# Three key loads of a decode-attention kernel, each issued when a small marker transfer ahead of it has landed

## Chip, cores, metric

One core of one Trainium2 chip. The metric is the device time of one execution in microseconds (us), median of several runs.

## The reference, cut to what matters

Two attention blocks with one query token each (B=4, 32 query heads, 8 key/value heads, head size 128), outputs side by side. Block A reads the whole cache of 8192 positions, block B the last 2048.

```python
q = (x @ wq).reshape(B, 1, 32, 128)                    # per block
scores = einsum("bhqd,bhkd->bhqk", q, k) * 128**-0.5   # k, v: each head serves 4 query heads
p = softmax(scores)
out = einsum("bhqk,bhkd->bhqd", p, v).reshape(B, 1, 4096) @ wo
```

Every key and value is used once, so the bytes of the caches are the work: 184.6 MB are read from HBM in all.

## The kernel before

The work is cut into 20 *units* of 4 MB of keys and 4 MB of values: units 0 to 3 for block B (one batch entry each), 4 to 19 for block A. Keys and values have two buffers each; unit u uses slot u % 2. Between them come 1 MB pieces of the output weights, `Wo`. SyncE issues nearly all transfers, in program order on one queue. Before each it waits until compute has freed the buffer.

```python
def kv_load(kind, u):                       # cut
    ...
    if un["P"] == 1:                        # block B: keys in 2 parts, values in 4 of 1 MB
        for q in range(NPART[kind]):
            ...
            op("sp", dma(buf[:, slot, q * n:(q + 1) * n, :], src), waits=w, inc=(...))
        return
    w = [("otr", u - 2)] if kind == "V" else [("otr", u - 3)] if u >= 2 * T0P else [...]
    ...
    op("sp", lambda sp: sp.sem_inc(sem, bump), waits=w, bump=(sem, bump, None))   # carries the wait
    ...
    op("sp", dma(buf[:, slot, :, :].rearrange("p t d -> p (t d)"), src), inc=(kind, u, 0))

kv_load("K", 0)
for u in range(1, NU + 1):
    if u < NU:
        kv_load("K", u)
    kv_load("V", u - 1)
    tn = u // 2
    if u % 2 == 0 and tn in pieces:         # one Wo piece in two units, u = 6, 8, ... 18
        ...
        op("sp", dma(Wo_sb[...], src), waits=[("ocp", tn - 1)], inc=("wo", tn))
    ...
# then eight loads of 128 KB, the last piece of wo, and the store of the result
```

A wait `("rs", 7)` or `("otr", 5)` is a semaphore wait on the issuing engine; a DMA counts its semaphore up by 16, one from each of the 16 DMA engines.

## Time and profile before

| | before |
|---|---|
| median of 4 runs | 439.17 us (439.14 to 439.53) |
| bytes moved, mean rate | 184.73 MB, 423 GB/s |
| last load landed, profiled run | 434.43 of 437.0 us |

The prediction below shows the slices, the waits and the order of issue. These are the DMA queues of the kernel before (packets, MB, share of the time of 16 engines):

```profile
q1 hardware_dynamic: 10960, 184.56, 99.1%
q8 instruction: 8, 0.13, 0.1%
q14 instruction: 4, 0.03, 0.0%
```

Twelve packets of 16 or 8 KB, a tenth of a per cent, belong to *instruction*: the fetching of the engines' programs. (The packet records have seven of the 16 KB packets between 25 and 71 us, the eighth at 431 us; of the 8 KB ones, one each at 63, 91, 160 and 289 us. Fetches from before the span's start are not on the page.)

### The profile page before, as it was taken

The page shows a single profiled execution, that of the slowest core. Times are in us where ns is not written, and L with a number is a line of the kernel's source. Part 1 is how long each engine was busy: PE and PEld are TensorE (multiplying, and loading weights), DVE is VectorE, ACT ScalarE, POOL GpSimd, SP SyncE. Part 2 cuts the span into 40 slices and gives each one's busy share as a digit, 9 for nine tenths or more (in the row PEclk, how much of TensorE's full clock was granted, in tenths as well). Part 3 has the DMA queues.
Part 4 walks back from the last instruction along what each step waited for, and adds up shares of the span by engine and source line. Part 5 has one row for each costly group of instructions (what it writes and reads, how often), then busy time and mean ns, then how long its engine had stood idle before and what let it go on. Part 6 is the DMA issues. An engine that isn't in the chain of part 4 may idle for free.

```text
span 437.0 us, 15525 instructions
## 1 busy us (share of the span) xinstructions
PE 365.0 (84%) x7174; PEld 337.9 (77%) x7184; DVE 210.0 (48%) x406; ACT 195.0 (45%) x249; POOL 27.7 (6%) x88
## 2 busy tenths in 40 slices
PE   0168898998998959895989598969868996989996
PEld 0158897997997949795979588868868886979975
DVE  0004455664564634563456247525643563455651
ACT  1024473573653625371634254434534462536530
POOL 6100000000000000000000000000100000000000
PEclk9999999999999988999999899989996999799999
DMA  8999999999999999999999999999999999999996
GB/s 340 430 421 421 429 412 430 418 439 412 445 432 432 424 438 432 432 432 432 432 432 429 432 432 430 431 433 432 410 454 432 432 432 432 432 432 411 447 407 255
DMA packets 10996, 184.73 MB, mean 423 GB/s; under 512 B 1236, under 2 KB 2280, under 8 KB 2408
## 3 DMA queue, kind: packets, MB, share of 16 engines
q1 hardware_dynamic: 10960, 184.56, 99.1%
q8 instruction: 8, 0.13, 0.1%
q14 instruction: 4, 0.03, 0.0%
q10 hardware_dynamic: 24, 0.01, 0.0%
HBM read 184.56 MB, written 0.01 MB: 422 GB/s over the span
## 4 chain that ended last, share of the span: by engine, by line
PE 54%; DMA 40%; issue 2%; DVE 1%; SPq 1%; ACT 1%
DMA K_sb<-in_A_k_cache_dram 29%; PE KT L283 27%; PE OT L338 11%; DMA K_sb<-in_B_k_cache_dram 7%; PE SB L322 5%; PE SA L322 4%; DMA V_sb<-in_A_v_cache_dram 4%; PE KT L396 4%; PE SA L350 1%; PE KT L338 1%; SPq L566 1%; DVE oacc L404 1%; PE KT L263 1%; ACT KT_sb L299 1%; DVE OS L501 0%
## 5 line engine op out<-in xcount | busy, mean ns | idle before, releaser
L283 PE MATMUL KT<-identf,K_sb 128*128 128x128 f32 x1280 | 207.6, 296 | 44.1 <-DMA K_sb<-in_A_k_cache_dram 30.7
L299 ACT ACTIVATE KT_sb<-KT 128x1024 bf16<-128x1024 bf16 (+1 forms) x192 | 165.1, 881 | 120.6 <-PE KT L283 120.6
L283 PEld LDWEIGHTS KT<-identf,K_sb 128*128 128x128 f32 x1280 | 147.6, 150 | 49.3 <-DMA K_sb<-in_A_k_cache_dram 31.7
L299 DVE COPY KT_sb<-KT 128x512 int32<-128x512 int32 x160 | 110.5, 691 | 132.1 <-PE KT L283 130.7
L338 PE MATMUL OT<-PT,V_sb 128*128 128x64 bf16 x2560 | 78.1, 193 | 1.6 <-issue 1.1
L338 PEld LDWEIGHTS OT<-PT,V_sb 128*128 128x128 bf16 x2560 | 75.9, 98 | 1.8 <-issue 1.2
L469 ACT ACTIVATE PT<-Dt 128x512 bf16<-128x512 f32 x40 | 24.6, 630 | 84.0 <-DVE Dt L458 84.0
L322 PEld LDWEIGHTS SA<-RQc,KT_sb 128*128 128x128 bf16 x1280 | 56.9, 98 | 2.3
L322 PEld LDWEIGHTS SB<-RQc,KT_sb 128*128 128x128 bf16 x1280 | 51.1, 97 | 7.9 <-issue 4.4
L322 PE MATMUL SA<-RQc,KT_sb 128*128 128x16 bf16 x1280 | 56.4, 170 | 0.0
L322 PE MATMUL SB<-RQc,KT_sb 128*128 128x16 bf16 x1280 | 52.9, 170 | 0.0
L420 DVE TENSOR_REDUCE M<-SB 128x8 f32<-128x512 f32 (+1 forms) x20 | 13.8, 692 | 50.0 <-PE SB L322 50.0
L441 POOL PARTITION_ALL_REDUCE MB<-M1m x20 | 7.7, 387 | 334.3 <-DVE M1m L434 334.3
L396 PE MATMUL KT<-Wo_sb,OL 128*4 128x512 bf16 x80 | 18.9, 379 | 0.0
L201 PE MATMUL KT<-ident,x_sb 4*128 4x4 bf16 x8 | 0.6, 170 | 19.9 <-POOL identf L537 19.9
L201 PEld LDWEIGHTS KT<-ident,x_sb 4*128 4x128 bf16 x8 | 0.4, 112 | 20.1 <-issue 20.1
L476 DVE TENSOR_REDUCE LB<-SA 128x8 f32<-128x512 f32 (+1 forms) x20 | 13.7, 684 | 2.8 <-PE SA L350 2.8
L458 DVE TENSOR_TENSOR Dt<-SA,MBm 128x512 f32<-128x512 f32 x20 | 13.8, 692 | 0.7
L367 DVE TENSOR_TENSOR ORx<-KT,MSK 32x1024 bf16<-32x1024 bf16 x10 | 12.1, 1211 | 3.3 <-PE KT L362 3.3
L458 DVE TENSOR_TENSOR Dt<-SB,MBm 128x512 f32<-128x512 f32 x20 | 13.6, 681 | 0.0
L420 DVE TENSOR_REDUCE M<-SA 128x8 f32<-128x512 f32 (+1 forms) x20 | 13.6, 681 | 0.0
L350 PE MATMUL SA<-PT,onesb 128*128 128x128 bf16 x168 | 12.7, 218 | 0.0
(69 smaller groups left out, 118.0 us busy)
## 6 DMA issues: line engine op xcount, KB each, us to landing
K_sb<-in_A_k_cache_dram SPq DMA_DIRECT2D x15, 4096.0 KB, 22.5
V_sb<-in_A_v_cache_dram SPq DMA_DIRECT2D x15, 4096.0 KB, 30.3
K_sb<-in_B_k_cache_dram SPq DMA_DIRECT2D x8, 2048.0 KB, 23.6
V_sb<-in_B_v_cache_dram SPq DMA_DIRECT2D x16, 1024.0 KB, 18.4
V_sb<-in_B_wq_dram SPq DMA_DIRECT2D x1, 4096.0 KB, 12.5
V_sb<-in_A_wq_dram SPq DMA_DIRECT2D x1, 4096.0 KB, 21.8
Wo_sb<-in_B_wo_dram SPq DMA_DIRECT2D x4, 1024.0 KB, 11.9
K_sb<-in_A_k_cache_dram SPq DMA_DIRECT2D x2, 2048.0 KB, 17.5
```

Source lines behind the costliest of these rows:

```text
L283: ins = pe.transpose(out=bkf[:, pi * 128:(pi + 1) * 128], in_=K_sbf[:, slot, t0:t0 + 2, :].rearrange("p t d -> p (t d)"), identity=identf[ ...
L299: ins = e.tensor_copy(out=d, in_=r) if eng == "dve" else e.activation(out=d, in_=r, func=ACTF.Copy)
L322: ins = pe.matmul(out=stb[:, t % NTH * C:(t % NTH + 2) * C], lhsT=ktv[:, pi, :, e], rhs=RQc[:, u % 2, t // TS, e, :], start=(e == 0), stop ...
L338: ins = pe.matmul(out=otb[:, s * NW:s * NW + w], lhsT=V_sb[:, slot, t, :], rhs=PT[:, slot, t * C:t * C + w], start=(j == 0), stop=(j == n ...
L350: ins = pe.matmul(out=SA[u % 2][:, s * NM:(s + 1) * NM], lhsT=onesb[:, :], rhs=PT[:, u % 2, c0:c0 + NM], start=(i == 0), stop=(i == n - 1))
L367: return dve.tensor_tensor(out=ORx[:, :, :, :], in0=bk[0:NR, 0:128].rearrange("p (i o r) -> p r o i", o=1, r=C).broadcast_to([NR, C, C, 12 ...
L396: ins = pe.matmul(out=bk[0:Bn, 0:D], lhsT=OL[:, i, :], rhs=Wo_sb[:, i, :], start=(i == 0), stop=(i == C - 1))
L420: return dve.tensor_reduce(out=M1[:, h * n:(h + 1) * n].rearrange("p (s h) -> p s h", h=C), in_=bank[:, :].rearrange("p (s j h) -> p s h j ...
L441: return pool.partition_all_reduce(MB[:, 0:n], M1m[:, 0:n], channels=128, reduce_op=ReduceOp.max)
L458: return dve.tensor_tensor(out=Dt[:, h * NTH * C:(h + 1) * NTH * C].rearrange("p (s j h) -> p s j h", s=Sh, h=C), in0=bank[:, :].rearrange ...
L469: return act.activation(out=PT[:, u % 2, a:b], in_=Dt[:, a:b], func=ACTF.Exp, scale=scale)
L476: return dve.tensor_reduce(out=LB[:, 0:n].rearrange("p (s h) -> p s h", h=C), in_=SA[u % 2][:, 0:NSEG * NM].rearrange("p (s j h) -> p s h ...
```

## The change

Three transfers of 1 KB are added. Each stands one 1 MB piece ahead of a key load, and that key load waits until the marker has landed. The intent is to have SyncE issue the key loads of units 5, 9 and 15 at a known place of the stream, with one piece of work still in the queue to cover the way to the first byte.

```diff
+        rs_sb = sb("rs_sb", [16, 32], BF16)
...
+        MARKS = (3, 7, 13)
+        marked = []
+        def mark(u):
+            if u in MARKS:
+                op("sp", dma(rs_sb[:, :], WO[0][0:16, 0:32]), inc=("rs", u))
+                marked.append(u)
+        def passed():
+            return [("rs", marked.pop())] if marked else []
...                                          # block B
-                        w = [("T", tjob_idx[(u - 2, 8 * q + 7)])] if u >= 2 else []
+                        w = ([("T", tjob_idx[(u - 2, 8 * q + 7)])] if u >= 2 else []) + passed()
...
+                        if q == NSEG - 1:   # before the last 1 MB of values
+                            mark(u)
...                                          # block A
-            op("sp", dma(buf[...], src), inc=(kind, u, 0))
+            op("sp", dma(buf[...], src), waits=passed() if kind == "K" else [], inc=(kind, u, 0))
...
             if u % 2 == 0 and tn in pieces:
                 P, q = pieces[tn]
+                mark(u - 1)                 # before the Wo piece
```

More of the change, by code (lines that the diff above doesn't have):

```diff
@@ L128, in bass_concat_heads__gqa_block_cached__sliding_block_cached__decode_kernel @@
                  "out0", "out1", "out2", "Tq", "Td", "Ta", "S", "PV", "Ed", "Ea", "Eq", "vs", "sub", "exp", "otr", "otp",
-                 "ocp", "Ef", "fin0", "fin1", "ar1", "SM", "msk", "pset", "setup", "pm0", "pm1", "oc", "ocB", "mkb", "perm", "rq"]
+                 "ocp", "Ef", "fin0", "fin1", "ar1", "SM", "msk", "pset", "setup", "pm0", "pm1", "oc", "ocB", "mkb", "perm", "rq", "rs"]
         sems = {n: sm("s_" + n) for n in names}
@@ L160, in sem_of @@
             return sems["vs" if t in ("max", "maxc", "sum", "rcp", "os") else t]
-        DMA_KEYS = ("K", "Kh", "KH", "V", "Vh", "VL", "WL", "x", "out", "WQ", "wo")
+        DMA_KEYS = ("K", "Kh", "KH", "V", "Vh", "VL", "WL", "x", "out", "WQ", "wo", "rs")
         plan = {e: [] for e in ("sp", "pe", "act", "dve", "pool")}
@@ L747, in kv_load @@
                 return
-            op("sp", dma(buf[:, slot, :, :].rearrange("p t d -> p (t d)"), src), inc=(kind, u, 0))
+            op("sp", dma(buf[:, slot, :, :].rearrange("p t d -> p (t d)"), src), waits=passed() if kind == "K" else [], inc=(kind, u, 0))
         for P in (1, 0):
```

## The prediction

> **What bounds the kernel now.** I read the page from the top: the busy shares, the slices, the DMA part; then the waits, the issues of SyncE in order of time, and single transfers. The busy shares do not point anywhere by themselves: TensorE is at 84%, VectorE at 48%. The slices do.
>
> ```profile
> PE   0168898998998959895989598969868996989996
> PEclk9999999999999988999999899989996999799999
> DMA  8999999999999999999999999999999999999996
> GB/s 340 430 421 421 429 412 430 418 439 412 445 432 432 424 438 432 432 432 432 432 432 429 432 432 430 431 433 432 410 454 432 432 432 432 432 432 411 447 407 255
> DMA packets 10996, 184.73 MB, mean 423 GB/s; under 512 B 1236, under 2 KB 2280, under 8 KB 2408
> ```
>
> The DMA row is full in 38 of 40 slices, at 432 GB/s, and only the first and the last are not. 184.73 MB at 432 GB/s is 427.6 us of a span of 437.0. TensorE has a hollow (a 5 or 6) in every fourth slice. The waits name it:
>
> ```profile
> PE KT L283 <- DMA K_sb<-in_A_k_cache_dram: 30.7, 8, 5.3
> SPq L566 <- DVE oacc L404: 137.0, 6, 23.8
> SPq L741 <- DVE ON L504: 94.6, 6, 16.5
> ```
>
> TensorE waits for a key load eight times, up to 5.3 us each (once in each pair of units of path A, which takes about 41.3 us). SyncE itself also waits long, for compute to free buffers, and yet the DMA row has no hole. So when SyncE issues there is still work in the ring. The next view is SyncE in order of time, around the second marker (start, duration):
>
> ```profile
> 159.25 0.54 SPq L566 DMA_DIRECT2D K_sb<-in_A_k_cache_dram  x1
> 159.89 0.55 SPq L566 DMA_DIRECT2D V_sb<-in_A_v_cache_dram  x1
> 183.97 0.33 SPq L566 DMA_DIRECT2D Wo_sb<-in_B_wo_dram  x1
> 184.48 0.54 SPq L566 DMA_DIRECT2D K_sb<-in_A_k_cache_dram  x1
> 201.46 0.54 SPq L566 DMA_DIRECT2D K_sb<-in_A_k_cache_dram  x1
> ```
>
> These are the keys of unit 8, values of 7, a piece of Wo (1 MB), keys of 9 and keys of 10; values of 8 (185.12) are left out. The time from issue to landing of three of them, in this order (values of 7, Wo, keys of 9):
>
> ```profile
> DMA to landing us min/median/max: 33.2/33.2/33.2
> ...
> DMA to landing us min/median/max: 11.6/11.6/11.6
> ...
> DMA to landing us min/median/max: 20.8/20.8/20.8
> ```
>
> So they land at 193.1, 195.6 and 205.3: in the order of issue, 2.5 us apart for 1 MB and 9.7 us for 4 MB, whatever the issue time. Counting bytes issued less bytes landed in the packet records, the ring holds 4.3 MB (10 us) when keys 9 are issued, and from the first load to about 410 us it never holds less than 3.06 MB (7.1 us). The kernel is a queue that never runs dry; its length is bytes over rate, plus about 2 us of start and about 3 us of tail.
>
> **What the Trainium skill says.** (1) "DMA: Bandwidth & Descriptors", section "Where 436 GB/s comes from", gives 16 ports at 850 MHz, 435.2 GB/s together. The trace agrees: 432. A packet of 32 KB takes 1211 ns at least, 1218 at the median and 1221 at the ninth decile, so there is no faster transfer to be had. (2) Same page, "Queues, rings and completion order": each of the 16 engines consumes its ring in order. The landings above agree, so a marker lands only when what was issued before it is through. (3) Same page, "Why a DMA increments its semaphore by 16 and not by 1": each engine that takes part counts up by itself, and only the sixteenth increment means landed. The trace shows how far apart they are: the 16 increments of values 7 come from 191.00 to 193.11, those of Wo from 193.50 to 195.59. The skew is a steady 2.1 us. The slowest engine decides. (4) Same page, "Latency and other measured facts", gives about 600 ns from a hardware-generated DMA to its first byte. This trace has more: first issue at 0.80, first packet at 1.84, 1.04 us later.
>
> **The change, part by part.**
>
> *Added instructions.* Three transfers of 16 rows of 64 bytes, one row per engine. A 512-byte packet takes 25 ns and a completion packet of 4 bytes 9 ns, so each marker costs an engine at most about 34 ns, 0.1 us for all three. On SyncE three more issues of about 0.35 us, in time in which it waited anyway.
>
> *Moved: the three key loads.* The order of all big transfers in the ring stays; only the time of issue moves.
> - Marker 1 stands before the fourth 1 MB piece of values 3. The third piece landed at 110.41; keys 5, issued at 98.80, now go out at about 110.5, 11.7 us later.
> - Marker 2 stands behind values 7 and before the Wo piece: keys 9 go from 184.48 to about 193.2, 8.7 us later.
> - Marker 3 stands behind values 13 (landing 317.16): keys 15 go from 308.05 to about 317.2, 9.2 us later.
>
> In each case exactly one piece of 1 MB lies behind the marker, 2.43 us of work. Question: is that enough to cover the way from the marker's landing to the first bytes of the keys?
>
> *The race, for marker 2.* The last engine's completion packet of values 7 is recorded at 192.65, its increment at 193.11 (0.46 later). With the marker's 0.03 and some 0.04 until SyncE goes on (estimate: other issues start 0.02 to 0.05 after the releaser's end), keys 9 issue at 193.18. That slowest engine finishes its share of Wo at 195.14. Slack: 1.96 us.
>
> How long does a transfer on an empty ring need? From the first transfer of the kernel: issued at 0.80, eight 32 KB packets per engine (8 x 1.218 = 9.74 us), increments from 12.52 to 13.32. Less 0.43 us from the last packet to its increment (at the end, 434.00 to 434.43), the data started as if at full rate at 2.35 to 3.15, so 1.55 to 2.35 us after issue, engine by engine. Against 1.96: the early engines' keys are there in time; the latest engine loses 2.35 - 1.96 = 0.39 us. The fast engines, up to 2.2 us ahead (dry at 192.93), do idle, for up to 1.8 to 2.6 us, but that spends their lead and not the end: everything waits for the sixteenth increment. The DMA row could show a small dent and the time nothing.
>
> The other two races have the same terms: last completion packet of the third piece at 109.98, of the fourth at 112.44; of values 13 at 316.69, of the Wo piece at 319.17. Slack about 1.9 to 2.0 us each.
>
> *Sum.* Per marker between 0 (warm, the descriptors come sooner than at the cold start) and 0.4 us; keys 5, 9 and 15 take 0.54 us to issue where the first transfer took 0.39, which might add 0.15 to the upper end. Three times: 0 to 1.6 us, plus 0.1 for the markers. No compute removed, so nothing is won. I take the middle, +0.7 us.
>
> *What is behind on SyncE.* It issues in order, so values 4 (105.95), 8 (185.12) and 14 (308.70) also move, to some 0.6 us after their keys. The next issue is at 123.99, 201.46 and 325.05, at least 7 us later, and waits for compute. With values and keys in the ring as before, the backlog at those points is as before (3.2 to 5.5 MB).
>
> **Rivals.**
> - *Real holes in the ring.* If a marker of 64-byte rows lands 1 us late, or a refill under load takes 3 us, each marker costs about 1.0 to 1.5 us on the slowest engine: +3 to +4.5 us, 442 to 444, still within 2%. For it: the first packets of the cold start took 1.7 to 2.2 us in place of 1.2. Against: the small store at the end lands 1.2 us after its issue, whole.
> - *The fast engines' idling pulls the mean down for good.* All engines move equal bytes; if lead and lag change hands from marker to marker, each hole hits a different slowest engine. The hole of the whole transfer is then the largest lateness, counted above as 0.4 to 0.55 us; at worst 3 x 0.8 = +2.4 us, 441.6.
> - *A gain.* A shallower ring would have to make packets shorter. The minimum lies 0.6% below the median: 2.5 us at the very most, 436.7. Nothing ties packet time to backlog: at 3 and at 10 MB the slices show the same 432 GB/s.
> - *The late keys hurt TensorE.* Keys 9 landed at 205.31 with 10 us in front of them. Unless the ring empties they land at the same time, and TensorE waits for them as before.
>
> **Range and chances.** 439.17 + 0.7 = 439.9 us. The low end, 439.0, is no hole and the best of the noise (439.14 to 439.53); the high end, 441.8, is three holes of about 0.8 us. Two per cent would be 8.8 us, 2.9 us per marker, more than the whole slack plus the refill of a cold start; slower by that 2%, faster 1%, within 2% the rest.
>
> **What would show it.** In the changed profile the keys of 5, 9 and 15 issue at about 110.5, 193.2 and 317, right behind a small transfer, with issue to landing of about 12 us in place of 20.8 to 23.8. Their landings, at 122.6, 205.3 and 329.3, should move by no more than the sum of the holes so far. SyncE should show three waits for the marker's DMA, of 8 to 12 us. The DMA row should stay at 9 and the increments of later transfers should lie closer together than 2.1 us, because the fast engines lost their lead. The prediction is wrong if keys 9 land later than 206.5, if the time falls below 438.5, or if later transfers are issued against an empty ring.

## The result and the profile after

443.01 us, median of 4 runs (442.86 to 443.08), against 439.17: a ratio of 1.0085 (95% interval 1.0068 to 1.0103). It lies within 2%, but outside the predicted range of 439.0 to 441.8. Ratios are the mean time of one kernel's runs over the mean of the other's of the same rounds, so not quite the ratio of the medians.

The page of the changed kernel:

```profile
DMA  8999999999999999999999999999999999999996
GB/s 336 426 425 421 430 413 431 417 438 412 379 428 428 424 441 440 437 398 428 428 428 428 428 428 443 434 443 434 400 414 428 428 428 428 434 431 425 437 421 231
DMA packets 11092, 184.74 MB, mean 419 GB/s; under 512 B 1332, under 2 KB 2376, under 8 KB 2504
```

At this grain there is almost nothing to see. Slices of 11 us still show a 9. Two rates dip at a marker (379 and 398, slices 11 and 18). The third marker's key load goes out at 319.86 us, as slice 30 begins, and that shows only 414; the 400 of slice 29 is no mark of it, since the kernel before has 410 there. The waits show what the change did to SyncE:

```profile
SPq L567 <- DMA rs_sb<-in_A_wo_dram: 30.0, 3, 12.7
PE KT L284 <- DMA K_sb<-in_A_k_cache_dram: 31.1, 10, 5.1
```

Three waits for the marker, 30.0 us in all, and TensorE's wait for keys hardly changed (30.7 us before). SyncE in order of time around the second marker, the same stretch as in the prediction:

```profile
162.41 0.55 SPq L567 DMA_DIRECT2D V_sb<-in_A_v_cache_dram  x1
163.01 0.58 SPq L567 DMA_DIRECT2D rs_sb<-in_A_wo_dram  x1
186.30 0.33 SPq L567 DMA_DIRECT2D Wo_sb<-in_B_wo_dram  x1
194.95 0.54 SPq L567 DMA_DIRECT2D K_sb<-in_A_k_cache_dram  x1
203.81 0.53 SPq L567 DMA_DIRECT2D K_sb<-in_A_k_cache_dram  x1
```

and from issue to landing, for the first four of these (values 7, marker, Wo, keys 9):

```profile
DMA to landing us min/median/max: 32.3/32.3/32.3
...
DMA to landing us min/median/max: 31.9/31.9/31.9
...
DMA to landing us min/median/max: 10.9/10.9/10.9
...
DMA to landing us min/median/max: 12.4/12.4/12.4
```

The landings are at 194.8, 194.9, 197.2 and 207.3. Keys 9 follow Wo by 10.1 us where it was 9.7 before: a hole of 0.4 us, as the prediction had it. Three holes of this size are 1.3 us; the loss is 3.8.

**Sixteen engines, not one queue.** The trace records each of the 16 increments of a transfer's semaphore. Sorted, and less the first of the sixteen, they show how far the engines are apart. Left: when the last one landed (from the traces' semaphore updates, not a view of the profile).

```
before
102.95  0.00 0.07 0.30 0.47 0.70 0.73 0.77 1.48 1.64 1.68 1.72 1.74 1.81 1.93 1.98 2.06   keys 4
154.25  0.00 0.06 0.34 0.50 0.70 0.72 0.78 1.51 1.66 1.69 1.73 1.76 1.81 1.96 2.01 2.09   first Wo piece
163.96  0.00 0.07 0.36 0.51 0.73 0.73 1.43 1.52 1.67 1.71 1.74 1.78 1.83 1.96 2.02 2.10   keys 7
205.31  0.00 0.04 0.29 0.50 0.68 0.70 1.43 1.47 1.65 1.67 1.72 1.75 1.79 1.95 2.01 2.08   keys 9
426.70  0.00 0.26 0.51 0.70 0.72 0.73 1.46 1.51 1.67 1.69 1.74 1.79 1.90 1.98 2.05 2.10   values 19, first part
434.43  0.00 0.46 0.64 0.67 0.68 1.29 1.34 1.47 1.49 1.55 1.59 1.67 1.69 1.78 1.84 1.88   last piece of wo
after
113.60  0.00 0.00 0.02 0.14 0.15 0.88 1.17 1.48 1.55 1.58 1.58 1.66 1.70 1.70 1.71 2.59   values 3, last piece
123.78  0.00 0.05 0.07 0.08 0.14 0.17 0.21 0.23 0.24 0.25 0.28 0.34 0.37 0.45 0.45 0.47   keys 5, first marker
165.56  0.00 0.03 0.03 0.07 0.13 0.16 0.21 0.22 0.23 0.24 0.34 0.35 0.44 0.45 0.46 0.90   keys 7
207.32  0.00 0.01 0.02 0.06 0.06 0.08 0.12 0.14 0.15 0.17 0.20 0.21 0.22 0.23 0.26 0.40   keys 9, second marker
278.31  0.00 0.00 0.01 0.06 0.06 0.08 0.09 0.12 0.14 0.20 0.21 0.21 0.24 0.26 0.41 0.90   values 11
332.23  0.00 0.03 0.21 0.24 0.27 0.31 0.32 0.36 0.38 0.38 0.39 0.40 0.40 0.41 0.42 0.45   keys 15, third marker
436.02  0.00 0.03 0.17 0.18 0.30 0.31 0.32 0.33 0.34 0.35 0.37 0.38 0.40 0.41 0.44 1.86   values 19, last part
438.65  0.00 0.06 0.14 0.16 0.26 0.27 0.28 0.29 0.30 0.31 0.32 0.33 0.34 0.35 0.36 1.58   last piece of wo
```

In the kernel before, six or seven engines run 1.3 to 2.1 us ahead of the slowest, and this *lead* lasts. It costs nothing, since the end is the slowest engine's. It also hides things: the 8 KB instruction packet at 159.76 us falls between the second and the third row, one engine goes from 0.78 to 1.43, and the last landing does not move. In the changed kernel the first marker closes the lead from 2.6 to 0.5 us (*levels* the engines): those that are ahead run dry and wait for the late keys. From then on they march together. And then *single* engines fall behind, by 0.5 us near 163 us, 0.5 near 275 and 1.4 near 434. Each time an instruction packet stands just before. For the last one, the DMA queues of the stretch 433.5 to 435.5 us of the changed kernel, then 431.0 to 432.5 of the kernel before:

```profile
q8 instruction: 1, 0.02, 3.4%
```

```profile
q8 instruction: 1, 0.02, 4.7%
```

Both kernels fetch 16 KB in the tail. The packet takes 1126 ns before and 1080 ns after (packet records); with what it delays around it, it puts one engine back by some 1.4 us. In the kernel before it falls on an engine that is ahead (six engines stand in front in the row of 426.70, five in that of 434.43), and the last landing doesn't move: the last 0.5 MB of values land 1.33 us after the part in front of them, after the change 2.73. The 8 KB packets near 160 and between 274 and 289 us take 309 to 318 ns, and the data packet behind lasts 1565 or 1566 ns (1628 at the later one) in place of 1218, in both kernels: 0.66 to 0.72 us for one engine.

The chain that ended last ends in this. Before, the last 16 matmuls on values run on without a break behind the others (x64 is 48 and these 16); after, TensorE starts them when the delayed engine's increment has come:

```profile
430.48 2.00 PE KT L338 x64
432.48 0.32 issue
432.79 0.27 PE KT L700
```

```profile
411.67 24.35 DMA V_sb<-in_A_v_cache_dram
436.02 0.05 issue
436.06 0.64 PE KT L339 x16
```

**Theory A**, then: a marker's wait costs about 0.4 us of *hole* (time in which even the slowest engine has nothing to move), and it levels the engines; later instruction fetches that fell on engines with a lead now fall on engines without one, and the end waits for each. **Rival B**: each marker is a hole in the queue of about 1.3 us, nothing else (3 x 1.28 = 3.84). **Rival C**: the 64-byte transfers themselves disturb the queue. **Rival D**: issuing late, with a shallow queue, costs by itself.

### The profile page after: what moved, and what is told of

Its sections match the earlier page's. It is cut to its first block, busy times and chain, and to the rows that moved or that the text cites. A ratio compares the mean times of both kernels' runs of the same rounds, so it can differ in the third digit from the quotient of the medians.

```text
span 441.3 us, 15538 instructions
## 1 busy us (share of the span) xinstructions
PE 367.7 (83%) x7184; PEld 339.5 (77%) x7184; DVE 209.8 (48%) x406; ACT 194.9 (44%) x249; POOL 27.6 (6%) x88
## 4 chain that ended last, share of the span: by engine, by line
DMA 47%; PE 39%; PEld 8%; issue 3%; SPq 1%; DVE 1%; PEldq 1%; ACT 0%
DMA K_sb<-in_A_k_cache_dram 20%; PE KT L284 20%; DMA rs_sb<-in_A_wo_dram 15%; PE OT L339 9%; DMA K_sb<-in_B_k_cache_dram 7%; DMA V_sb<-in_A_v_cache_dram 6%; PE SB L323 3%; PEld KT L284 3%; PE SA L323 3%; PEld OT L339 1%; PE KT L397 1%; PEld SA L323 1%; SPq L567 1%; PE KT L264 1%; PE SA L351 1%
```

## The experiments

Twelve runs, each with its own median and ratio to the kernel before (runs of the same rounds, 9 of them per call). The runs came on three chips (e1, e2, e3 and e5; e4, e6, e7 and e8; e9 to e12), with medians of the kernel before of 439.33, 439.03 and 439.33; the ratios are what can be compared.

| run | what | median us | ratio, 95% interval |
|---|---|---|---|
| e1_no_wait | markers, nobody waits | 439.31 | 0.9999 (0.9985 to 1.0013) |
| e2_two_ahead | all three wait, 2 MB behind the marker | 439.49 | 1.0004 (0.9991 to 1.0018) |
| e3_only_first | first marker | 441.10 | 1.0040 (1.0026 to 1.0054) |
| e4_only_second | second marker | 440.98 | 1.0041 (1.0027 to 1.0055) |
| e5_only_third | third marker | 441.20 | 1.0044 (1.0031 to 1.0058) |
| e9_third_quarter_more | third marker, 1.25 MB behind | 440.50 | 1.0024 (1.0010 to 1.0038) |
| e10_third_none_behind | third marker, nothing behind | 443.56 | 1.0095 (1.0080 to 1.0111) |
| e6_one_engine | change + 34 KB on one DMA engine | 443.33 | 1.0094 (1.0078 to 1.0109) |
| e7_all_engines | change + 34 KB on each | 444.30 | 1.0125 (1.0109 to 1.0140) |
| e8_before_one_engine | before + 34 KB on one engine | 439.67 | 1.0012 (0.9999 to 1.0026) |
| e11_change_again | the change again | 443.05 | 1.0084 (1.0070 to 1.0098) |
| e12_before_again | before again | 439.45 | 0.9998 (0.9985 to 1.0012) |

All gave the right result.

**The markers without their waits.**

```diff
-            return [("rs", marked.pop())] if marked else []
+            return []
```

> The three markers are issued, but no key load waits for them. Theory A (the marker waits level the 16 DMA engines: about 0.4 us of hole each, and afterwards an instruction fetch that falls on one engine is no longer hidden by that engine's lead): time as the kernel before, 439.2 us, within 0.3; the lead of the fastest engine stays near 2.1 us through the trace. Rival B (each marker costs a hole in the ring of about 1.3 us, nothing else): also 439.2. Rival C (the small marker transfer itself disturbs the ring, for instance its 64-byte writes): 443.0 as with the change.

439.31 us. The lead of the fastest engine is 2.0 us at 91 us and 2.4 at the end. The transfers themselves cost nothing that shows: rival C falls.

**Two pieces ahead instead of one.**

```diff
-                        if q == NSEG - 1:
+                        if q == NSEG - 2:
                             mark(u)
...
+            if kind == "V" and u in MARKS:   # values in 3 MB and 1 MB, the marker between
+                for i, (t0, t1) in enumerate(((0, NT - NT // 4), (NT - NT // 4, NT))):
+                    if i:
+                        mark(u)
+                    op("sp", dma(buf[:, slot, t0:t1, :]..., part), inc=...)
+                return
...
-                mark(u - 1)
```

> The key loads still wait for the markers and are issued 6 to 9 us later than in the kernel before, but 2 MB instead of 1 MB lie behind each marker (values of units 7 and 13 in two transfers of 3 and 1 MB, the marker between them; for unit 3 one piece earlier). Theory A: the keys reach the ring about 2.2 us after issue with 4.4 us of work left on the slowest engine and 2.2 on the fastest, so no hole and no levelling: 439.2 us within 0.3, lead near 2.1 us to the end. Rival B (holes alone): 439.2 too. Rival D (a late issue or a shallow ring costs by itself): 440.5 to 443.

439.49 us. The three waits are there (22.1 us in all). Keys 15 go out at 315.10 instead of 308.05 and land at 329.6 (329.3 before). The lead is 1.8 us at the end. Here a late issue, with 2 MB left in the queue, was free while every engine still had work: rival D falls. A and B both allow this run.

**One marker at a time.**

```diff
-        MARKS = (3, 7, 13)
+        MARKS = (3,)          # e4: (7,)   e5: (13,)
```

> Only the first marker with its wait. Theory A: hole 0.45, the fetch near 160 us exposed with about 0.45, the one near 280 us hidden behind it, the 16 KB one near 432 us exposed with 0.6 to 1.0: together 1.5 to 1.9, 440.7 to 441.1 us. Rival B: a third of the loss of the change, 1.28, 440.45 us, with the keys of unit 5 landing 1.3 us late and nothing lost later.

> Only the second marker with its wait. Theory A: hole 0.4 at the keys of unit 9, the fetch near 280 us exposed with about 0.5, the 16 KB one near 432 us with 0.7 to 1.1: together 1.6 to 2.0, 440.8 to 441.2 us; the three single markers then add up to more than the three together (5 to 5.7 against 3.84). Rival B: 1.28, 440.45 us, and the three singles add up to 3.84.

> Only the third marker with its wait. Theory A: until 319 us as the kernel before, the fetches near 160 and 280 us hidden; hole 0.4 to 0.5 at the keys of unit 15, then the 16 KB fetch near 432 us exposed with 1.3 to 1.5: together 1.7 to 2.0, 440.9 to 441.2 us. Rival B: 1.28, all of it at the keys of unit 15: 440.45 us.

441.10, 440.98 and 441.20. The three excesses are 0.40, 0.41 and 0.44%, together 1.25%, or 5.5 us of 439.2; all three markers in one kernel cost 0.85%, 3.7 us. Costs of their own would add up; these don't, because one levelling is enough to expose the tail's fetch, and the later levelling pays for it again only in part. That speaks against B and for A. The traces say where the time went. The step is by how much the last landing moves against the first trace of before:

| step, us | change | change again | first only | second only | third only |
|---|---|---|---|---|---|
| up to keys 4, before any marker | 0.72 | 0.34 | 0.74 | 0.70 | 0.36 |
| hole at keys 5 | 0.46 | 0.52 | 0.42 | | |
| 8 KB fetch near 162 us | 0.45 | 0.44 | 0.54 | 0.00 | 0.00 |
| hole at keys 9 | 0.42 | 0.49 | | 0.55 | |
| 8 KB fetch, 275 or 290 us | 0.50 | 0.56 | 0.06 | 0.49 | 0.00 |
| hole at keys 15 | 0.38 | 0.42 | | | 0.96 |
| 16 KB fetch near 433 us | 1.28 | 1.33 | 0.78 | 0.56 | 0.83 |
| holes / fetches | 1.26 / 2.23 | 1.43 / 2.33 | 0.42 / 1.38 | 0.55 / 1.05 | 0.96 / 0.83 |

A fetch counts only after a levelling (the zeros), and a later fetch counts only for what it exceeds the largest lag so far. The last fetch is read at the first of the eight 128 KB loads that shows it; at the eighth it is 1.32 and 1.22 in the two traces of the change, and 0.77, 0.57 and 0.86 with one marker. With the third marker alone the hole was larger than expected (0.96 for 0.4 to 0.5, with one engine 0.4 us behind the others) and the fetch smaller (0.83 for 1.3 to 1.5): that run met its expected total, but not its parts. The first line is no effect of the change; before again has 0.49 there: at 91 us an 8 KB fetch falls now on an engine that is ahead, now on one that is last.

**The same wait without a hole.** This separates the two parts of A. With 1.25 MB behind the marker the slowest engine should never run dry, but the fast ones should.

```diff
-        MARKS = (3, 7, 13)
+        MARKS = (13,)
...                                          # as e2, with values 13 in 3.75 and 0.25 MB
+                for i, (t0, t1) in enumerate(((0, NT - NT // 16), (NT - NT // 16, NT))):
```

> Only the third marker, with 1.25 MB behind it instead of 1 MB (values of unit 13 in two transfers of 3.75 and 0.25 MB, the marker between). The slowest engine then has about 3.04 us of work after the marker has passed it, and the keys reach the engines 2.3 to 2.8 us after that moment. Theory A: no hole on the slowest engine (keys of unit 15 land with the kernel before, within 0.15), but the fast engines still idle and keep a lead of only 0.3 to 0.8 us, so the 16 KB instruction fetch near 432 us is exposed with 0.7 to 1.3: 439.8 to 440.5 us, all of the loss after 430 us. Rival B (holes alone): no hole, no loss: 439.2.

440.50 us, at the upper end of A's numbers. Keys 15 were issued at 316.83, and this is their time to landing:

```profile
DMA to landing us min/median/max: 12.6/12.6/12.6
```

That is 329.4: no hole (0.04 us against before). Yet the lead has shrunk, from 1.80 us at the Wo piece in front to 0.54 at keys 15, and then the fetch comes, in the stretch from 430.8 us:

```profile
q8 instruction: 1, 0.02, 4.0%
```

The increments of the last loads spread by 1.82 us, one engine alone behind, and 1.26 us of the loss appear there, of 1.39 in all at the last load. A wait that made the slowest engine lose nothing cost 1.1 us. Rival B expected 439.2 and falls.

**Nothing behind the marker.**

```diff
-        MARKS = (3, 7, 13)
+        MARKS = (13,)
...
-                mark(u - 1)
                 ...
                 op("sp", dma(Wo_sb[...], src), waits=[("ocp", tn - 1)], inc=("wo", tn))
+                mark(u - 1)
```

> Only the third marker, now behind the Wo piece, so that nothing lies behind it. The ring empties. Theory A: hole on the slowest engine = 0.5 us until SyncE issues + up to 2.25 us until data flow at full rate = 2.7 to 2.8, then the 16 KB fetch with 1.3 to 1.5: together 4.0 to 4.3, 443.2 to 443.6 us. Rival B with a fixed cost of 1.28 for each marker: 440.45; rival B with a hole that grows with the missing work: 2.43 more than 1.28, 3.7, all of it at the keys of unit 15.

443.56 us: a hole of 2.84 at keys 15 and 1.32 at the fetch. The row of the stretch 317 to 323 us (the last figures are the DMA engines' share and the rate, which count a packet where it starts), for the kernel before, third only, 1.25 MB and nothing behind, in this order:

```profile
317.00:323.00 6.00, 5.93 (x154) 5.61 (x154) 3.33 (x9) 2.28 (x3) 0.37 (x1) 1.00 1.07 459
```

```profile
317.00:323.00 6.00, 6.00 (x132) 5.58 (x131) 3.28 (x5) 3.53 (x4) 0.00 (x0) 1.00 0.91 352
```

```profile
317.00:323.00 6.00, 5.93 (x154) 5.61 (x154) 3.32 (x9) 2.26 (x3) 0.37 (x1) 1.00 1.10 440
```

```profile
317.00:323.00 6.00, 5.93 (x144) 5.60 (x144) 3.32 (x7) 2.85 (x3) 0.37 (x1) 1.00 0.46 175
```

The hole follows the work behind the marker: none, 1 and 1.25 MB gave 2.84, 0.4 to 1.0 (1.56 in one trace below) and 0.04 us. The cost of the fetch does not follow it: 1.32, 0.83 and 1.26.

**A lag put in by hand.** If a lead hides a fetch, so must a lag: one engine made 1.4 us late on purpose should hide the tail's fetch on another one.

```diff
+        ex_sb = sb("ex_sb", [128, 2176], BF16)
...
             if u == 16:
+                exs = KC[0][0, 0, :, :]
+                op("sp", dma(ex_sb[0:17, 0:1024], AP(exs, [[1024, 17], [1, 1024]])), inc=("ex", 0))
                                             # e7: ex_sb[0:128, :], AP(exs, [[2176, 128], [1, 2176]])
...
-        op("sp", dma(out[:, 0, 0:H2], ...), waits=[("ocp", NTURN)], ...)
+        op("sp", dma(out[:, 0, 0:H2], ...), waits=[("ex", 0), ("ocp", NTURN)], ...)
```

> The changed kernel plus one load of 34 KB on 17 partitions into a scratch buffer at about 352 us, after the third marker; all of it should go to one DMA engine (17 packets of 2 KB, about 1.4 us). Theory A: that engine then trails by 1.4 us, the 16 KB instruction fetch near 434 us falls on another one and no longer counts: 443.0 within 0.3. If by chance it falls on the same engine: 444.4. Rival B, where the end is holes that all engines share: every later landing waits for that engine, 444.4 us.

> The changed kernel plus a load of 557 KB on 128 partitions at the same place, 34 KB for each of the 16 engines. Both theories: 1.3 to 1.5 us later, 444.3 to 444.5. It is the control for the one-engine load.

443.33 and 444.30 us, the first just above what was expected. In the one-engine run 17 packets of 2 KB took 1.57 us together, on one engine. The increments, in the same form as above:

```
364.19  0.00 0.00 0.02 0.04 0.05 0.06 0.14 0.14 0.17 0.18 0.22 0.23 0.29 0.33 0.34 0.64   before the extra load
375.10  0.00 0.01 0.02 0.03 0.05 0.18 0.20 0.21 0.29 0.31 0.31 0.34 0.38 0.39 0.61 1.67   after it
437.54  0.00 0.01 0.02 0.05 0.06 0.20 0.23 0.25 0.28 0.30 0.31 0.34 0.39 0.40 0.63 1.60
438.01  0.00 0.03 0.03 0.07 0.19 0.23 0.23 0.28 0.28 0.31 0.33 0.38 0.40 0.62 1.56 1.71   after the fetch
438.87  0.00 0.02 0.04 0.06 0.16 0.20 0.21 0.24 0.26 0.28 0.29 0.31 0.33 0.57 1.48 1.50   last piece of wo
```

The load put one engine back and the last landing with it, by 1.21 us. The fetch then put a second engine back to the same place, and the last landing moved by 0.01. Two lags, one price: the same fetch moved the last landing by 1.2 to 1.3 us in the change. In time, the 34 KB on one engine cost 0.4 us by the ratios (1.0094 against 1.0085 and 1.0084), which is within the intervals; the control cost 1.8 by the ratios (1.0125), 1.3 by the medians. But the times alone show little here, since the control is not a clean one: in its trace the third refill put three engines 0.7 to 1.1 us behind the rest, a hole of 1.56 us (0.78 in the one-engine run), and its tail fetch cost 0.28 for that reason. Both runs also have 0.35 us at keys 10 that the other traces do not have. I do not know the cause of either. What carries the point is the step of 0.01 in the trace.

> The kernel before plus the one-engine load of 34 KB at about 350 us. Theory A: the kernel before has six engines 1.4 to 2.1 us ahead and ten within 0.7 us of the slowest. If the engine is one of the six: 439.2 within 0.2. If it is one of the ten: 0.7 to 1.4 us later, 439.9 to 440.6. Rival B says nothing of leads: 440.6.

439.67 us, 0.5 more by the ratio, whose interval reaches down to no loss. That is neither of the two times that A had named. The last landing moved by 0.47 at this load. By the increments (one fewer near 1.0, one more near 2.5) the load fell on an engine that was about 1.3 us ahead of the slowest, neither the front nor the rear. 17 packets of 1.67 us together less this lead leave 0.4, near the 0.47; that the lead paid for the rest is this reading of one trace.

**Both kernels again.**

> The changed kernel once more (only a comment differs), for a second trace and a tighter ratio: 443.0 within 0.3. Theory A: again three holes of 0.4 to 0.5 at the keys of units 5, 9 and 15, about 0.45 after each of the 8 KB fetches near 163 and 275 us and 1.3 to 1.5 after the 16 KB fetch near 434 us. What the two traces have before the first marker may differ by chance.

> The kernel before once more (only a comment differs), for a second trace: 439.2 within 0.3. Its landings should show how far the time before the first marker moves by chance: the keys of unit 4 land at 102.95 in the first trace of before and at 103.67 in that of the change.

443.05 and 439.45 us. The second trace of the change repeats the first step by step (table above).

What none of this does is to move an instruction fetch at will. But the fetches moved by themselves, and the lag moved with them. The 16 KB packet started at 433.82 and 433.86 us in the two traces of the change, at 433.01, 433.20 and 432.24 with one marker, at 431.09 with 1.25 MB and at 434.79 with nothing behind. The first late landing is that of values 19 in one of them and of the first to the fourth of the eight last loads in the others, and it comes 2.20 to 2.39 us after the packet's start in all seven. The 8 KB packet at 274.68 or 274.45 (the change) delays values 11; where it comes at 289.76 (second only), values 11 are on time and values 12 late. So that the three lags are the fetches' work rests on this, on the packet records (size, the stretched data packet behind), and on the lag by hand behaving alike. The records do not name the DMA engine of a packet; that packet and lag belong to the same engine is inferred.

## Why the prediction was wrong

- *Bound, order of transfers, times of issue*: right. Keys 5, 9 and 15 went out at 111.35, 194.95 and 319.86 (predicted 110.5, 193.2 and 317.2, plus what was lost by then), 12.4 us before they landed.
- *The hole*: right at the upper end. From the two traces of the change 0.38 to 0.52 us each, 1.3 to 1.4 in all, against 0 to 1.6. In other traces the third hole was larger than the 0.8 of the range's end (0.96 alone, 1.56 in the control), so that this size is not settled. The keys flow at full rate 1.75 to 2.26 us after their issue; the prediction took 1.55 to 2.35 from the cold start.
- *The markers' own cost*: right, nothing visible.
- *The failed step* is this: the fast engines "do idle, for up to 1.8 to 2.6 us, but that spends their lead and not the end: everything waits for the sixteenth increment." True at that moment, and false for what comes after. The lead was what hid the three later fetches; without it they cost 2.2 to 2.3 us. The sum had no such term. Holes 1.26 to 1.43 and fetches 2.23 to 2.33 are 3.5 to 3.8; counted at the very last load, the two traces lose 3.50 and 3.59 us after keys 4, against 3.84 between the medians. The rest stands before the first marker (0.72 and 0.34, against 0 and 0.49 in the kernel before), where the two traces of one kernel differ by as much.
- The rival of *real holes* named the time that was measured (442 to 444), but by a mechanism that the traces do not show: holes of 1.0 to 1.5 us each, where the change had 0.38 to 0.52.
- The rival that the fast engines' idling pulls the time down "for good" came near, but looked for the loss in the holes themselves, "at worst 3 x 0.8".
- One comparison in it is wrong: 2.9 us per marker is not more than the slack plus the refill of a cold start, 1.96 and up to 2.35. With no slack at all the hole was 2.84.
- The prediction did foresee that the increments would lie "closer together than 2.1 us", and named keys 9 landing later than 206.5 as what would refute it. They landed at 207.3 (207.0 in the second trace).

## What to carry to other kernels

In these traces a stream over 16 DMA engines behaved as 16 queues, and the lead of the faster ones as a cushion: a delay of one engine that was shorter than that engine's own lead was free. A wait for the landing of a recent transfer made the fast engines idle until the slowest had caught up and so spent the cushion. Leave more work behind the marker than the refill time plus the engines' spread (an estimate from the 2.3 and 2.1 us here: 4.4 us, or 1.8 MB at 2.43 us for each; 2 MB were enough, 1.25 MB not, though the slowest engine lost nothing). When the time is bytes over rate, read the sixteen increments of a landing, not only the last one.

## What the Trainium skill lacked or had wrong

- "Runtime: NRT & Kernel Launch", section "Instruction fetch mechanics", says that a program is fetched in blocks of 16 KiB by a DMA queue of the sequencer, and that the cost of crossing a block is one tail update, "mostly hidden". The traces agree on the 16 KB packets, but not that the cost stays hidden: a packet of 1080 to 1138 ns in the tail put one engine of the data's 16 back by about 1.4 us, and the kernel by 1.2 to 1.3 us in the change, where that engine had no lead. Packets of 8 KB (309 to 318 ns) are there too, and cost 0.44 to 0.56 us. No page has these prices.
- "DMA: Bandwidth & Descriptors", section "Queues, rings and completion order", has a ring of its own for each engine, and each engine shares its time between queues; the increments agree with both. It does not say that the engines' spread lasts. It stayed at 2.0 to 2.1 us from 50 to 430 us in the first trace of the kernel before, and no page names it as something to keep.
- Same page, "Latency and other measured facts": about 600 ns to the first byte. First packet here 1.04 us after issue, and full rate after 1.75 to 2.26 us on a queue that just ran dry. No page has a figure for how much work must be left behind to refill without a hole: 1 MB left holes of 0.4 to 1.6 us, 1.25 MB 0.04, and nothing 2.84.
